# Identity matmuls in TensorE's early gaps: attention with normalized q and k, then a hard-swish feed-forward

## The chip, the cores and the metric

The kernel runs on one core of one Trainium2 chip. The metric is device time in microseconds (us), lower is better. The kernel before took 438.7 us, the median of three runs that lie between 438.64 and 440.98. Engines are named as in the profile: PE is TensorE's matmuls, PEld its weight loads, DVE VectorE, ACT ScalarE, POOL GpSimd, SP the queue that issues most transfers; a small q behind a name (SPq, POOLq) is that engine's queue of transfers.

## The reference

```python
def rmsnorm(x, g):
    rms = np.sqrt(np.mean(x * x, axis=-1, keepdims=True) + 1e-06)
    return x / rms * g
q_n, k_n = (rmsnorm(q, g_q), rmsnorm(k, g_k))
scores = scale * np.matmul(q_n, k_n.transpose(0, 1, 3, 2))
scores = scores - np.max(scores, axis=-1, keepdims=True)
attn = np.exp(scores)
attn = attn / (np.sum(attn, axis=-1, keepdims=True) + 1e-09)
attn_out = np.matmul(attn, v)
x = attn_out.transpose(0, 2, 1, 3).reshape(B * S, H * D)
h = x @ w_in
g = h * np.clip(h + 3.0, 0.0, 6.0) / 6.0
out = g @ w_out
```

There are 8 batches, 12 heads, 448 positions and a head size of 64, so x is 3584 x 768; w_in is 768 x 2048 and w_out 2048 x 768. Inputs and output are 32-bit floats; the kernel's matmuls take bf16.

## The kernel before

**Attention.** Work goes by pairs of heads: 6 pairs a batch, 48 in all. q and k of two pairs are loaded together into one of three buffers (`kq_in`), v into one of three (`v_st`). For a pair, squares are made on ACT or POOL (`square`, L331 and L334), summed on DVE (`stats_sum`, L337), turned into a factor on ACT (`stats_rstd`, L345 and L348) and multiplied in, nearly always on POOL (`normalize`, L353). PE transposes the pair (`transposes`, L367, eight matmuls with the identity), DVE or ACT copies the two halves out of the accumulators (`put_q` L385, `put_k` L303). From pair 14 on transposing DMAs do that instead. Scores are matmuls of 448 columns into two accumulator buffers `sc` (`burst` L395, `rests` L402), ACT takes the exponential into `eT` (L408), PE weighs v with it (`weigh`, L429 and L435: per tile one matmul of 130 columns and six of 65, each with its own 128x128 weight load), DVE divides (`divide`, L445 and L446). v is first cast into `vaug` (`cast_v`, L303 or L307) on whichever engine the planner picks. The result is transposed (`x_out`, L464, or a DMA, L468) and copied into `xT` (L475).

**Feed-forward.** For a batch whose x is complete, `h_mm` (L479) multiplies w_in with `xT`, six matmuls of 448 columns for each of 16 blocks of d_ff; ACT and DVE apply the gate (L485, L490); `y_mm` (L498) multiplies with w_out. One block is special: `h_early` (L588) computes the first block of the first batch piece by piece, one matmul as each pair's x arrives, into the accumulator bank `m_r[0]` (profile name `m`). A bank has 512 columns of 32 bits, of which every user takes columns 0 to 447 or fewer. Pair transposes of x of the first batch go to the other bank, `m_r[1]`.

**What sets the order.** The order of every engine's instructions is fixed when the program is built. `Plan.run` (L140) steps a clock of its own, in ns, over the operations that are ready, with a planned price for each, and calls for each engine the one with the lowest key; what it calls is emitted in that order. Feed-forward matmuls stand in two lanes (`h`, `y`) and are taken when PE has nothing of attention to do or when a credit has run out. Each engine then runs its list in order, and waits by semaphores for the operands. PE is filled from pairs, from `h_early`, and later from the lanes; until the first batch's x is complete there is nothing in the lanes, and the planned clock jumps on (`if not best: now = min(soon)`, L171).

**Weights.** They are loaded by POOL's queue: w_in in five loads (`load_w_in`, L313), the first three after the third group of pairs, w_out in four (L318). POOL's list has its normalizations, squares and casts between these.

**The identity.** POOL makes it at the start (`make_identity`): a memset and one select that ends 2.39 us after the span's start.

Of the kernel before, what the change touches and what calls it, by code (L numbers as in the profile page):

```python
# [28 lines left out]
class Op:  # L29
# [4 lines left out]
    def __init__(self, key, ways, deps, lag, size):  # L34
        self.key, self.ways, self.lag, self.size = key, ways, lag, size
        self.deps = {id(d): d for d in deps if d is not None}
        self.next, self.end, self.time = [], None, 0.0
        self.early = {}
        self.load = False
        self.bank = None  # L40
        self.readers = []
        for d in self.deps.values():
            d.next.append(self)
        self.left = len(self.deps)
# [19 lines left out]
class Plan:  # L64
# [6 lines left out]
    ISSUE, LAND, RATE = {"SP": 600, "ACT": 600, "POOL": 900}, 1700, 270.0  # L71

    STEADY, SLACK, EARLY = 110e3, 500, 3000

    def __init__(self, share):
        self.free = {e: 0.0 for e in ("PE", "ACT", "DVE", "POOL", "SP", "pipe")}
        self.known, self.todo = [], 0
        self.lanes, self.row, self.banks = {"h": [], "y": []}, [], []
        self.share, self.credit = share, 0.0

    def add(self, key, ways, deps=(), lag=0, size=0, hold=False):
        op = Op(key, ways, deps, lag, size)
        op.left += hold
        self.todo += 1
        if op.left == 0:
            self.known.append(op)
        return op
# [52 lines left out]
    def run(self):  # L140
        now = 0.0
        while self.todo or self.row or any(self.lanes.values()):
            soon = [t for t in self.free.values() if t > now]
            best = {}
            for op in self.known:
                t = op.time
                if op.bank is not None:
                    free = After(op.bank).end
                    if free is None:
                        continue  # L150
                    t = max(t, free + self.HOP)
                if t > now:
                    soon.append(t)
                    continue
                engine, ns, fn = min(op.ways, key=lambda w: max(self.free[w[0]], now) + w[1] * (
                    self.PRICE.get(w[0], 1.0) if op.key[0] >= self.FAIR else 1.0))
                if self.free[engine] <= now and (engine not in best or op.key < best[engine][0].key):
                    best[engine] = (op, ns, fn)
            if self.free["PE"] <= now and ("PE" not in best or self.credit < 0):
                if not self.row:  # L160
                    pick = self.next_item(now, soon)
                    if pick:
                        it, bank = pick
                        for lane in self.lanes.values():
                            if lane and lane[0] is it:
                                lane.pop(0)
                        it.bank, bank[1] = bank, it.out
                        self.row = list(it.ops)
                if self.row:
                    best["PE"] = (self.row[0], *self.row[0].ways[0][1:])  # L170
            if not best:  # L171
                now = min(soon)
            for engine, (op, ns, fn) in best.items():
                if op.key is None:
                    self.row.pop(0)
                    share = next((self.share[i] for i in range(0, len(self.share) - 1, 2)
                                  if it.place < self.share[i + 1]), self.share[-1])
                    self.credit = min(self.credit + ns * share, 2000.0)
                else:
                    self.known.remove(op)  # L180
                    self.todo -= 1
                    if engine == "PE":
                        self.credit = max(self.credit - ns, -2000.0)
                self.begin(op, engine, ns, fn, now)
        return now
# [3 lines left out]
def kernel(  # L189
# [11 lines left out]
    nc = tc.nc  # L201

    B, H, S, D = q.shape
# [26 lines left out]
    identity = const.tile([P, P], BF16, name="identity")  # L230
# [29 lines left out]
    plan = Plan(share=(2.0, 1.0, 0.65, 3.0, 0.45))  # L260
# [217 lines left out]
    def h_mm(b, f, kt, m):  # L478
        nc.tensor.matmul(  # L479
            out=m[:, 0:S], lhsT=w_in_sb[:, kt, f * P:(f + 1) * P], rhs=xT[:, kt, b % NX, x_slot(b)],  # L480
            start=(kt == 0), stop=(kt == NKT - 1),
        )

    def relu(m, t):
        nc.scalar.activation(  # L485
            out=t[:], in_=m[:, 0:S], func=RELU, bias=0.5, scale=1.0 / 6.0,
        )

    def gate(b, f, m, t):
        nc.vector.scalar_tensor_tensor(  # L490
            out=gT[:, f, (b % 2) * S:(b % 2 + 1) * S], in0=t[:], scalar=1.0,
            in1=m[:, 0:S], op0=A_MIN, op1=A_MULT,
        )
# [60 lines left out]
    nrm, vc, tr, pq, pk, wgh, div, xo, px = ([] for _ in range(9))  # L554
# [19 lines left out]
    def h_item(b, f):  # L574
        deps = [w_in_op(f)] + px[HP * b:HP * b + HP]

        deps += y_ops.get(b - 2, [])[-1:] + (y_rest.get(b - 1, []) if b % 2 == 0 else [])
        it = plan.item("h", b + f / NFT, NKT, 189, lambda kt, m: h_mm(b, f, kt, m), deps)
        h_ops.setdefault(b, []).append(it.ops[-1])
        n = len(gate_ops)  # L580
        t = t_r[n % len(t_r)]
        r = add((0, 0), [("ACT", 550, lambda: relu(it.bank[0], t))],
                [it.ops[-1]] + gate_ops[n - len(t_r):n - len(t_r) + 1] * (n >= len(t_r)))
        it.out = add((0, 0), [("DVE", 600, lambda: gate(b, f, it.bank[0], t))], [r])
        gates.setdefault(b, []).append(it.out)
        gate_ops.append(it.out)

    def h_early(f):  # L588

        m, t, mm = m_r[f], t_r[f], None  # L590
        for kt in range(NKT):
            mm = add((kt + 2, 2), [("PE", 189, lambda kt=kt: h_mm(0, f, kt, m))],
                     [px[kt], mm, w_in_op(f)], 165)
        h_ops.setdefault(0, []).append(mm)
        r = add((0, 0), [("ACT", 550, lambda: relu(m, t))], [mm])
        out = add((0, 0), [("DVE", 600, lambda: gate(0, f, m, t))], [r])
        gates.setdefault(0, []).append(out)
        gate_ops.append(out)
        plan.banks.append([m, out])
# [23 lines left out]
    def feed_forward(b):  # L623

        if b:
            ts = (NT, *range(NT)) if b % 2 == 0 else range(NT)
            ys = [(t, c) for t in ts for c in range(DM // YC)]
            if b == 1:
                ys = [(0, 0), (1, 0), (0, 1), (1, 1), (2, 0), (2, 1)]
            for i, (t, c) in enumerate(ys):  # L630
                last = b == B and t == NT - 1
                for j in range(2 if last and c else 1):
                    n = YC // 2 if last and c else YC
                    y_item(b - 1, t, c * YC + j * n, n, b + YLAG + (i + j / 2) / len(ys), last)
        if b < B:
            for f in range(NFT):
                h_early(f) if b == 0 and f < 1 else h_item(b, f)
# [20 lines left out]
    def w_in_op(f):  # L658
        return next(op for end, op in w_in_ops if f * P < end)
# [16 lines left out]
    for p in range(NPAIR):  # L676
        g = p // GP
        if p % GP == 0:
# [21 lines left out]
            for i in range(GP):  # L700
                j, p0 = min(i, len(todo) - 1), p + i
                parts = []
                for part in ((0, 1) if p0 == 0 else (2,)):
                    m = len(squares)
# [133 lines left out]
```

## Time and profile before

| what | value |
|---|---|
| median of three runs | 438.7 us |
| the profiled execution | 439.38 us |
| its span, first to last instruction | 437.6 us |
| mean granted TensorE clock, as recorded | 0.996 |
| matmuls, busy PE | 3520, 409.8 us |
| first matmul on PE | 9.38 us |
| POOL busy from 20 to 40 us | 19.88 of 20 us |
| DMA traffic in all | 64.55 MB, 148 GB/s on average |

The profile shows one execution, in microseconds from the first instruction. A row of the timeline gives start, duration, engine, line, operation, result and operands, the number of instructions merged, and in brackets how long the engine had been idle and what released it. Matmuls overlap, so that their durations include the way through the array; the distance from one start to the next is what a matmul costs in a stream. PEclk is the clock that a throttle granted to TensorE, where it is recorded. Idle time of an engine that nothing waits for costs nothing.

### The profile page before, as it was taken

To read this page: it belongs to the slowest core of one execution; us is meant where nothing else is said; L and a number is where in the kernel's file an instruction comes from. 1 tells how busy PE (TensorE), PEld (TensorE's weight loads), DVE (VectorE), ACT (ScalarE), POOL (GpSimd) and SP (SyncE) were. 2 spreads that over 40 slices of the span, in tenths; PEclk is the share of its full clock that TensorE was granted. 3 is DMA by queue.
4 is the path that set the end of the run, shared out by engine and by line. 5 is a ranking of instruction groups with operands and counts; after the bars stand their busy time and mean duration, and the time that the engine had idled before them with its cause. 6 is when DMAs were issued, how large, how long until landed. Compare 5 with 4: busy or idle time off the path is not lost.

```text
span 437.6 us, 8944 instructions
## 1 busy us (share of the span) xinstructions
PE 409.8 (94%) x3520; PEld 236.5 (54%) x3520; DVE 234.7 (54%) x492; ACT 254.3 (58%) x414; POOL 195.2 (45%) x146
## 2 busy tenths in 40 slices
PE   0677899999999998999999999999999999999997
PEld 0355565555566554555555555555565555555565
DVE  6486777766455557556466366344444253343322
ACT  3886887734877885968778587666643032132100
POOL 3697785596377776859676556311000000000000
PEclk9998999999999999999999999999999999999999
DMA  6999999995978898999999994333211201100022
GB/s 170 267 228 216 221 222 239 250 190 131 237 161 190 204 217 189 201 219 194 227 212 167 191 213 121 73 88 91 61 24 49 72 1 51 59 36 37 25 85 73
DMA packets 126506, 64.55 MB, mean 148 GB/s; under 512 B 77824, under 2 KB 123008, under 8 KB 126464
## 3 DMA queue, kind: packets, MB, share of 16 engines
q1 hardware_dynamic: 117488, 57.24, 57.5%
q0 software_dynamic: 8144, 6.29, 9.2%
q8 instruction: 27, 0.44, 0.4%
q10 hardware_dynamic: 832, 0.46, 0.4%
q14 instruction: 15, 0.12, 0.1%
HBM read 45.61 MB, written 11.01 MB: 129 GB/s over the span
## 4 chain that ended last, share of the span: by engine, by line
PE 82%; DMA 7%; ACT 3%; DVE 3%; SPq 2%; POOL 2%; issue 1%; ACTq 0%; POOLq 0%
PE m L479 18%; PE m L498 17%; PE t_ps L498 9%; PE t_ps L479 8%; PE av L435 7%; PE sc L395 6%; PE sc L498 6%; PE sc L479 4%; DMA kq_in<-in_k_dram 3%; DMA kq<-qk 3%; PE av L429 2%; DMA kq_in<-in_q_dram 2%; PE sc L402 2%; ACT eT L408 2%; DVE ssq L337 1%
## 5 line engine op out<-in xcount | busy, mean ns | idle before, releaser
L408 ACT ACTIVATE eT<-sc 128x896 bf16<-128x896 f32 x168 | 147.2, 915 | 42.2 <-PE sc L395 38.5
L498 PEld LDWEIGHTS <-gT 128*128 128x128 bf16 x912 | 85.5, 98 | 61.7 <-issue 8.9
L479 PE MATMUL m<-xT,w_in_sb 128*128 128x448 bf16 x486 | 109.9, 353 | 1.7 <-DVE xT L475 0.6
L479 PEld LDWEIGHTS <-w_in_sb 128*128 128x128 bf16 x768 | 70.7, 98 | 68.8 <-issue 12.0
L353 POOL TENSOR_TENSOR qk<-kq_in,rstd 128x1024 bf16<-128x1024 f32 x47 | 89.0, 1903 | 41.6 <-DMA kq<-qk 20.8
L498 PE MATMUL m<-w_out_sb,gT 128*128 128x384 bf16 (+1 forms) x480 | 87.3, 324 | 0.0
L334 POOL TENSOR_TENSOR sq<-kq_in 128x1024 f32<-128x1024 f32 x41 | 77.2, 1894 | 13.0 <-DMA kq_in<-in_q_dram 3.6
L490 DVE SCALAR_TENSOR_TENSOR gT<-t_sb,m 128x448 bf16<-128x448 f32 x81 | 49.9, 618 | 41.8 <-ACT t_sb L485 41.4
L485 ACT ACTIVATE t_sb<-m 128x448 f32<-128x448 f32 x81 | 44.1, 546 | 47.9 <-PE m L479 47.2
L337 DVE TENSOR_REDUCE ssq<-sq 128x16 f32<-128x1024 f32 (+1 forms) x49 | 58.1, 1190 | 9.5 <-POOL sq L334 7.5
L435 PE MATMUL av<-vaug,eT 128*128 128x65 bf16 x1152 | 59.6, 196 | 0.0
L435 PEld LDWEIGHTS <-eT 128*128 128x128 bf16 x1152 | 52.8, 100 | 7.2 <-issue 1.6
L498 PE MATMUL t_ps<-w_out_sb,gT 128*128 128x384 bf16 x256 | 46.9, 326 | 0.0
L395 PE MATMUL sc<-kq 64*128 64x448 bf16 x288 | 41.6, 363 | 4.0 <-ACT eT L408 2.5
L429 PE MATMUL av<-vaug,eT 128*128 128x130 bf16 x192 | 43.0, 224 | 2.4 <-ACT eT L408 1.2
L479 PE MATMUL t_ps<-xT,w_in_sb 128*128 128x448 bf16 x192 | 44.5, 352 | 0.7 <-DVE gT L490 0.7
L303 POOL CAST vaug<-v_st 128x512 bf16<-128x512 f32 x33 | 20.3, 620 | 55.0 <-PE av L435 46.6
L445 DVE RECIPROCAL rden<-av 128x4 f32<-128x4 f32 x96 | 17.3, 180 | 48.8 <-PE av L435 47.1
L446 DVE TENSOR_TENSOR xn<-av,rden 128x256 bf16<-128x256 f32 x96 | 40.7, 424 | 3.3
L374 ACT ACTIVATE kq<-kq,gprime 128x448 bf16<-128x448 bf16 x34 | 22.8, 670 | 14.2 <-DMA kq<-qk 14.2
L498 PE MATMUL sc<-w_out_sb,gT 128*128 128x384 bf16 (+1 forms) x176 | 29.1, 319 | 0.0
L485 ACT ACTIVATE t_sb<-t_ps 128x448 f32<-128x448 f32 x32 | 17.5, 547 | 19.7 <-PE t_ps L479 18.5
(50 smaller groups left out, 225.0 us busy)
## 6 DMA issues: line engine op xcount, KB each, us to landing
v_st<-in_v_dram SPq DMA_DIRECT2D x24, 384.0 KB, 4.7
kq_in<-in_k_dram SPq DMA_DIRECT2D x23, 384.0 KB, 4.5
kq_in<-in_q_dram SPq DMA_DIRECT2D x23, 384.0 KB, 4.8
out_dram<-y_sb SPq DMA_DIRECT2D x23, 384.0 KB, 2.6
w_out_sb<-in_moe_w_out_dram POOLq DMA_DIRECT2D x4, 768.0 KB, 19.1
w_in_sb<-in_moe_w_in_dram POOLq DMA_DIRECT2D x3, 768.0 KB, 16.2
out_dram<-y_sb SPq DMA_DIRECT2D x9, 192.0 KB, 2.7
v_st<-in_v_dram SPq DMA_DIRECT2D x48, 32.0 KB, 4.3
```

What stands on the lines that cost most here:

```text
L334: eng.tensor_tensor(out=sq, in0=x, in1=x, op=A_MULT)
L337: nc.vector.tensor_reduce(out=ssq_r[(p // GP) % 2][:, p % GP, :, which(part)].rearrange("p h a t -> p h (a t)"), in_=sq_r[m][:, :, which(p ...
L353: eng.tensor_tensor(out=qk_r[p % NQ][:].rearrange("p a t h d -> p h (a t) d"), in0=raw(p, 2), in1=rstd_r[(p // GP) % 2][:, p % GP].rearran ...
L395: nc.tensor.matmul(out=sc[:, h, 0:S], lhsT=kT_r[p % NK][rows, t * P:(t + 1) * P], rhs=qT_r[p % NK][rows], start=True, stop=True,)
L408: nc.scalar.activation(out=e2_r[d % NE][:, :, 0:S], in_=sc_r[i][:, :, 0:S], func=EXP, bias=0.0, scale=1.0,)
L429: nc.tensor.matmul(out=av, lhsT=rest[:, cols], rhs=va[:, 3].rearrange("p h d -> p (h d)"), start=True, stop=False, skip_group_check=True,)
L435: nc.tensor.matmul(out=av[:, h * W:(h + 1) * W], lhsT=e[t][h][:, cols], rhs=va[:, t, h], start=False, stop=(t == NT - 1 and h == 1), skip_ ...
L446: nc.vector.tensor_tensor(out=xn_r[p % NQ][:, t].rearrange("p n (h d) -> p n h d", h=2), in0=av4[:, :, :, 0:D], in1=rden.unsqueeze(3).to_b ...
L479: nc.tensor.matmul(out=m[:, 0:S], lhsT=w_in_sb[:, kt, f * P:(f + 1) * P], rhs=xT[:, kt, b % NX, x_slot(b)], start=(kt == 0), stop=(kt == N ...
L485: nc.scalar.activation(out=t[:], in_=m[:, 0:S], func=RELU, bias=0.5, scale=1.0 / 6.0,)
L490: nc.vector.scalar_tensor_tensor(out=gT[:, f, (b % 2) * S:(b % 2 + 1) * S], in0=t[:], scalar=1.0, in1=m[:, 0:S], op0=A_MIN, op1=A_MULT,)
L498: nc.tensor.matmul(out=m[:, 0:n], lhsT=gT[:, f, c0:c0 + P], rhs=w_out_sb[:, f, c:c + n], start=(f == 0), stop=(f == NFT - 1),)
```

## The change

The planner gets a filler. From 3000 ns of its own clock on, and until the last matmul of `h_early` has been planned, whenever PE is free and no operation is ready for it, the planner emits one matmul of the identity with 64 columns of the identity, and counts PE busy for 56 ns (before 6000 ns of the planned clock) or 36 ns (after). Its result goes to columns 448 to 511 of the bank that `h_early` uses, which nothing reads. The flag `start` is set until the first pair's x is planned, and not after.

```diff
+    WARM = 3000
...
+        self.fill = self.cold = None
...
                 if self.row:
                     best["PE"] = (self.row[0], *self.row[0].ways[0][1:])
+            if "PE" not in best and self.free["PE"] <= now and now >= self.WARM and self.cold.end is None:
+
+                self.fill()
+                self.free["PE"] = now + (56 if now < 2 * self.WARM else 36)
+                soon.append(self.free["PE"])
             if not best:
                 now = min(soon)
...
+    def fill(m, first):
+
+        nc.tensor.matmul(out=m[:, S:S + D], lhsT=identity[:], rhs=identity[:, 0:D], start=first, stop=False,
+                         skip_group_check=True)
...
         h_ops.setdefault(0, []).append(mm)
+        plan.fill, plan.cold = lambda: fill(m, px[0].end is None), mm
```

In the built program this adds 578 matmuls, each with a weight load of the identity, to PE's list. The order of all other instructions, on PE and on the other engines, is as before. The added ones stand, by number: 94 ahead of the first transposes; 34 after them; 42 after the first scores; 33 after the second pair's transposes; 33 ahead of the first `rests`; 52 ahead of the first `weigh`; 50 ahead of the first `x_out`; and 240 in smaller groups of 1 to 26 up to the `rests` that run at 48.62 us in the profile of before.

## The prediction

> **What bounds the kernel now.** I read the page first: TensorE's share, then its slices.
>
> ```profile
> PE 409.8 (94%) x3520; PEld 236.5 (54%) x3520; DVE 234.7 (54%) x492; ACT 254.3 (58%) x414; POOL 195.2 (45%) x146
> ...
> PE   0677899999999998999999999999999999999997
> ...
> PEclk9998999999999999999999999999999999999999
> ```
>
> TensorE ends the kernel: from slice 6 on it hardly rests, and the waits of PE show 4.7 us of idle time after 50 us, all before 227 us. The change touches only the first five slices (0 to 48.6 us), where PE waits. What counts is therefore how much sooner PE reaches the dense phase, which begins with the six matmuls at 52.42 us.
>
> Next the table by stretches of 3.41 us, laid to the one change of clock that is recorded. (Columns: stretch, length, busy time and count of PE, PEld, DVE, ACT, POOL, granted clock, DMA share, GB/s.)
>
> ```profile
> 18.09:21.50 3.41, 2.45 (x24) 1.63 (x25) 1.32 (x3) 3.09 (x7) 3.41 (x3) 1.00 1.07 280
> 21.50:24.91 3.41, 2.89 (x39) 2.50 (x38) 2.89 (x7) 2.44 (x6) 3.41 (x2) 1.00 1.02 264
> ...
> 31.74:35.15 3.41, 1.96 (x27) 1.29 (x27) 2.23 (x5) 3.04 (x4) 3.41 (x3) 1.00 1.16 185
> 35.15:38.57 3.42, 2.93 (x30) 2.33 (x28) 1.52 (x6) 1.25 (x2) 3.40 (x4) 0.50 1.28 226
> ```
>
> One stretch is recorded at clock 0.50: 35.15 to 38.57. It follows a stretch with PE busy for 1.96 of 3.41 us (57%). The clock before 24.91 is printed as 1.00, but the durations deny it:
>
> ```profile
> 23.84 0.54 PE L435 MATMUL av<-vaug,eT 128*128 128x65 bf16 x6
> 24.19 0.30 PE L429 MATMUL av<-vaug,eT 128*128 128x130 bf16 x1
> ```
>
> ```profile
> 32.16 0.35 PE L435 MATMUL av<-vaug,eT 128*128 128x65 bf16 x6
> 32.36 0.22 PE L429 MATMUL av<-vaug,eT 128*128 128x130 bf16 x1
> ...
> 37.11 0.55 PE L479 MATMUL m<-xT,w_in_sb 128*128 128x448 bf16 x1 [0.49 <-DMA w_in_sb<-in_moe_w_in_dram]
> 37.45 1.06 PE L367 MATMUL t_ps<-identity,qk 128*128 128x128 bf16 x8
> 38.31 0.48 PE L479 MATMUL m<-xT,w_in_sb 128*128 128x448 bf16 x1
> 38.72 0.55 PE L395 MATMUL sc<-kq 64*128 64x448 bf16 x4
> 39.21 0.23 PE L429 MATMUL av<-vaug,eT 128*128 128x130 bf16 x1
> ```
>
> From one start to the next, six matmuls of 65 columns, each with its weight load, take 0.35 us at first (58 ns each) and 0.20 us later (33 ns). So PE ran at half clock from 9.38 to 24.91 and from 35.15 to 38.57. Stretches with 85% and 86% busy were followed by full clock, those with 72% and 57% by half.
>
> Last, who else is at its limit before 52 us:
>
> ```profile
> 17.46:28.72 11.26, 8.96 (x102) 6.07 (x101) 7.69 (x18) 9.83 (x17) 11.17 (x6) 1.00 0.99 254
> 28.72:40.90 12.18, 9.50 (x107) 6.18 (x107) 8.45 (x21) 8.53 (x15) 12.16 (x12) 0.86 1.13 207
> ```
>
> POOL is busy for 11.17 of 11.26 and 12.16 of 12.18 us. It issues w_in's first load at 28.72, and PE waits for that load until 37.11. Whatever PE gains earlier is lost in that wait.
>
> **Part by part.** The change removes nothing and moves nothing: the order on all engines is the same but for 578 pairs (weight load of the identity, matmul of 64 columns) among PE's instructions. The nearest row is the 65-column matmul: 33 ns at full, 58 ns at half clock, so 19 to 34 us of new PE work in all.
>
> *First run, 94 fills.* They need only the identity, done at 2.39 us. 94 x 58 ns = 5.5 us ends at 7.8 us, before the first transposes at 9.38. On the path: nothing. The clock should rise during it; 7.8 to 9.38 then stays empty, which can cost one more half-clock stretch, since 57% busy was enough to lose the clock.
>
> *194 fills, 10.2 to 19.05* (34, 42, 33, 33, 52). The gaps of before are 1.16 + 0.94 + 0.39 + 1.18 + 1.07 = 4.74 us. At full clock the fills take 6.4 us, but the real work between saves 4 x 0.4 = 1.6 us. ACT hides more: its squares at 14.22 start when their DMA lands, and it is busy almost without a break to 20.36. One half-clock stretch of 3.41 us holds 59 fills, not 103, so PE loses 1.5 us inside it. I take 0.1 us late for POOL's start at 17.46 (bounds 0 and 1.0).
>
> *290 fills after 19.05.* At full clock av, scores and transposes end sooner than the fills need, up to 37.11, where PE waits 0.49 us anyway. Gain 0: POOL and the load cover it. The new instructions must also be fetched: PE's 7,040 came in the 27 packets of q8, about 260 each, so the change adds 4.4 packets of 1.0 us. At 54.16 and 65.32, where two of them ran, PE shows no idle time; I take 0 (bounds 0 and 1.0, one stall ahead of 19 us). Without that cover the half-clock PE pieces of the chain from 19.05 to 24.82, about 4.8 us of PE, would give back 2.4.
>
> *The stretch 35.15 to 38.57.* The gaps ahead of it (0.43, 0.48, 0.16) get 20, 15 and 9 fills, so PE stays above 85% and the clock should hold. From 37.11 to 38.72 PE does two matmuls of 448 columns (0.39 and 0.41 by their starts) and 8 transposes (0.81): 1.61 us, half of it saved, 0.8. ACT was waiting for just this:
>
> ```profile
> 39.13 2.54 ACT L408 ACTIVATE eT<-sc 128x896 bf16<-128x896 f32 x3 [2.73 <-PE sc L395]
> ...
> 43.90 0.62 POOL L303 CAST vaug<-v_st 128x512 bf16<-128x512 f32 x1 [3.00 <-PE av L435]
> 44.98 3.76 POOL L353 TENSOR_TENSOR qk<-kq_in,rstd 128x1024 bf16<-128x1024 f32 x2 [0.45 <-ACT rstd L348]
> ...
> 48.70 3.74 POOL L334 TENSOR_TENSOR sq<-kq_in 128x1024 f32<-128x1024 f32 x2
> ```
>
> POOL now waits 3.00 us for PE, so the 0.8 passes to 43.90, to 44.98 and to 48.70. Late next is the q load that 48.70 reads: it landed at 47.82, a cap of 0.88. Then sums on VectorE, the gate, and PE at 52.42; the later chain runs from PE to PE and shifts with it.
>
> *Fills after 37.11.* 21 fills (0.69 us) stand in a gap of 0.30, 24 (0.79) in one of 0.60; POOL's 0.45 us wait for ACT hides most. I take 0.15 (bounds 0 and 0.4).
>
> *Two rules weighed.* The row first: the clock fell after a stretch whose longest gap was 0.48 us. The Trainium skill, TensorE: Matmul & The Clock Gate, section "What's actually happening", lets it fall after at least one idle window of about 3.4 us; by that rule idle gaps were not the cause, fills could not hold the clock, and the 0.8 drops out. The trace speaks against it. And 65 columns with their weight load took 33 ns; the same page, "Back-to-back issue gap", gives about 81 ns a matmul for streams of 128 columns with weight loads; as an estimate by that figure the 194 fills would take 15.7 us, and the sum would be some 9 us slower.
>
> **Sum.** -0.8 + 0.1 + 0.15 = -0.55 us. The profiled execution took 439.38 us (span 437.6 and 1.78 around it), so 438.83. The median of the three runs shown is 438.7, 0.68 lower; with the same shift that is 438.15, rounded to **438.2**.
>
> **Rivals.**
> 1. *The clock falls anyway, or the cap comes earlier.* For: the empty 7.8 to 9.38 shows that the plan's gaps aren't the chip's. Against: 85% busy was enough twice. Then only the costs are left: 438.7 + 0.25 = 438.95. The first rule weighed above ends here too.
> 2. *One late half-clock stretch between 10 and 19 us.* POOL has no slack to 40.9, so its bound of 1.0 goes through: 438.7 + 1.0 + 0.15 - 0.8 = 439.05 with the later gain, 439.9 without.
> 3. *Fills outlast their gaps, slower.* It decides where the 194 fills stand: gaps 4.74, savings 1.6, and 1.0 of slack behind av (ACT idle 0.28 at 20.64, av and scores 0.74 sooner) give 7.3 us, or 38 ns a fill. At 33 they fit; at 58, if the small matmuls don't raise the clock, they don't. With 0.86 for transposes and 0.75 for scores at half clock, PE would be 0.64 late at 11.57, 2.0 at 13.44, some 2.6 at the scores that ACT needs at 16.13, 5.6 at 19.05. POOL would be late by 2.6 at 17.46 and about 4.3 at 26.88, which waits for ACT: 443.0 (442 to 445).
> 4. *POOL isn't the bound and PE's half clock is.* The chain of waits does run through PE from 19.05 to 24.82: -2.4 beside the -0.8 gives 435.5. Against: POOL's 11.17 of 11.26.
>
> **How the numbers follow.** Forecast 0.62, first rival 0.14, second 0.09, third 0.10, fourth 0.05. A measurement of this kernel can tell about 0.5% (2.2 us) from no change: the first three cases lie within it (0.85), the fourth above, the fifth below. The range goes down to 437.2 (438.7 less the cap of 0.88, less 0.6 of the 0.68 by which two executions of before differ) and up to 441.0 (the second rival's 439.9 and 1.1 more, about the slowest run shown, 440.98; that holds a fetch stall too). It holds the first three cases; the third and fourth rivals stay outside.
>
> **What would show it.** Right: 65-column matmuls at 33 ns from about 15 us on; no 0.50 from 30 to 40 us; POOL's normalization still near 17.46 and w_in's wait still ending near 37.1; the scores at 38.72 near 37.9; the dense phase near 51.8. Wrong: fills at 58 ns after 16 us, scores of 16.13 late by more than 0.3, w_in landing later, or the first matmul of w_in moved well ahead of 37.

## The result and the profile after

The changed kernel took **443.13 us**, the median of 12 runs (440.6 to 449.0), against 439.38 us for the kernel before in 12 runs beside it (437.48 to 442.32). The ratio is 1.0073, with a 95% interval from 1.0045 to 1.0101; it is worked out without the one execution of 449.0, which ran in a slower state, and is not the quotient of the two medians. The kernel is slower, and outside the range of the prediction. The profiled execution took 445.28 us with a span of 443.5, so 5.9 us more span than before; it lies 2.15 above its median, and the accounts below are those of this one execution.

From the page of the changed kernel: TensorE's share, its slices and clock, and the queue that carries instructions (packets, MB, share of 16 engines).

```profile
PE 424.0 (96%) x4098; PEld 252.9 (57%) x4098; DVE 235.1 (53%) x492; ACT 254.1 (57%) x414; POOL 195.1 (44%) x146
...
PE   6888899999999998899999999999999999999996
...
PEclk9999989999999999999999999999999999999999
...
q8 instruction: 32, 0.52, 0.5%
```

The same queue on the page of the kernel before:

```profile
q8 instruction: 27, 0.44, 0.4%
```

PE is busier in the first slices, as meant: 578 matmuls more. The dip of the clock has moved, from slice 4 to slice 6. Five more packets of instructions came, each of 16,384 bytes, and these turn out to matter.

PE's timeline of the changed kernel (start, duration, line, operation, operands, count, idle time and its releaser):

```profile
2.44 5.20 PE L493 MATMUL m<-identity 128*128 128x64 bf16 x94 [2.44 <-POOL identity masks.py:199]
9.17 0.62 PE L374 MATMUL t_ps<-identity,qk 128*128 128x128 bf16 x8 [1.53 <-DVE qk L360]
...
17.62 1.68 PE L493 MATMUL m<-identity 128*128 128x64 bf16 x52
19.21 0.23 PE L436 MATMUL av<-vaug,eT 128*128 128x130 bf16 x1
...
38.97 0.36 PE L486 MATMUL m<-xT,w_in_sb 128*128 128x448 bf16 x1 [0.68 <-DMA w_in_sb<-in_moe_w_in_dram]
...
39.96 0.55 PE L402 MATMUL sc<-kq 64*128 64x448 bf16 x4
...
55.67 2.23 PE L486 MATMUL m<-xT,w_in_sb 128*128 128x448 bf16 x6 [2.39 <-DVE gT L502]
```

The fills cost what was predicted: the first 94 end at 7.64, and the 52 from 17.62 to 19.21 take 31 ns each. PE is 0.16 us late at 19.21 against 19.05. But the wait for w_in ends at 38.97 instead of 37.11, and the six matmuls that open the dense phase come at 55.67 instead of 52.42, after a wait of 2.39 us. Among PE's waits the profile names none for instructions.

POOL's timeline of the changed kernel, and after it three rows of the kernel before:

```profile
17.62 1.90 POOL L360 TENSOR_TENSOR qk<-kq_in,rstd 128x1024 bf16<-128x1024 f32 x1
21.01 1.89 POOL L341 TENSOR_TENSOR sq<-kq_in 128x1024 f32<-128x1024 f32 x1 [1.48 <-PE t_ps L374]
...
30.27 2.54 POOL L320 DMA_DIRECT2D w_in_sb<-in_moe_w_in_dram  x3
...
51.94 3.74 POOL L341 TENSOR_TENSOR sq<-kq_in 128x1024 f32<-128x1024 f32 x2 [1.94 <-DVE kq L310]
```

```profile
17.46 1.90 POOL L353 TENSOR_TENSOR qk<-kq_in,rstd 128x1024 bf16<-128x1024 f32 x1 [0.27 <-ACT rstd L348]
19.32 1.90 POOL L334 TENSOR_TENSOR sq<-kq_in 128x1024 f32<-128x1024 f32 x1
...
28.72 2.54 POOL L313 DMA_DIRECT2D w_in_sb<-in_moe_w_in_dram  x3
```

POOL's normalization starts at 17.62, 0.16 later than before, but the square that followed it without a pause now waits 1.48 us. The brackets name PE and, later, VectorE, as the last event seen; the landings say otherwise. The q load that the square at 21.01 reads landed at 20.80 (before: 18.93), 0.21 us ahead of it. In four of the experiments below (e3, e4, e7, e8) the same square also starts 0.21 us behind this load, and in e8 the bracket names it. The one that the square at 51.94 reads landed at 51.78 (before: 47.82). From the first comes w_in's issue, 1.55 us late, and so the 38.97. From the second comes the 55.67, over VectorE's sum and the gate that stands behind it; VectorE's timeline of the changed kernel:

```profile
53.87 1.22 DVE L344 TENSOR_REDUCE ssq<-sq 128x16 f32<-128x1024 f32 x1 [2.07 <-POOL sq L341]
55.00 1.14 DVE L502 SCALAR_TENSOR_TENSOR gT<-t_sb,m 128x448 bf16<-128x448 f32 x2
```

So **loads land late**. What stands beside the step is the second packet of instructions, which ran at 16.94 for 1.23 us. SP's queue at that time in the changed kernel, and the same two issues before; then the queues of the changed kernel from 16.5 to 18.5 (packets, MB, share of 16 engines):

```profile
16.55 2.01 SPq L307 DMA_DIRECT2D v_st<-in_v_dram  x2
```

```profile
15.97 1.25 SPq L300 DMA_DIRECT2D v_st<-in_v_dram  x2
```

```profile
q1 hardware_dynamic: 842, 0.46, 92.7%
q8 instruction: 1, 0.02, 3.9%
```

A single packet of 16 KB takes 3.9% of 16 engines for 2 us, as much as one engine for 1.25 us, while the loads' packets take 93%. (Such shares add up packets that overlap, so that they can pass 100%.) On the trace, four of the loads' packets of 768 bytes that began beside it, at 17.05, 17.11, 17.21 and 18.11, took 0.58, 0.70, 1.27 and 0.38 us, where the median of the others is 0.036. By themselves these four prove little: in the kernel before, with no instruction packet near, five packets that began between 17.4 and 18.2 took 0.42 to 0.75 us, and in the changed kernel one at 13.05 took 1.06. What stands out is the step in the landings, and SP's issue: the k load due at 17.29 landed 1.95 us late, the one due 0.26 ahead of it 0.54 late, and SP's second issue took 1.37 us instead of 0.61.

### The profile page after: what moved, and what is told of

It reads as the page before. It is cut to its first block, busy times and chain, and to the rows that moved or that the text cites. A ratio compares the mean times of both kernels' runs of the same rounds, so it can differ in the third digit from the quotient of the medians.

```text
span 443.5 us, 10100 instructions
## 1 busy us (share of the span) xinstructions
PE 424.0 (96%) x4098; PEld 252.9 (57%) x4098; DVE 235.1 (53%) x492; ACT 254.1 (57%) x414; POOL 195.1 (44%) x146
## 4 chain that ended last, share of the span: by engine, by line
PE 74%; DMA 13%; SPq 5%; DVE 3%; POOL 2%; issue 1%; ACT 1%; ACTq 0%; POOLq 0%
PE m L486 17%; PE m L510 17%; PE t_ps L510 9%; PE t_ps L486 7%; PE sc L510 6%; PE av L442 6%; DMA kq_in<-in_q_dram 5%; PE sc L402 5%; DMA kq<-qk 4%; PE sc L486 4%; DMA v_st<-in_v_dram 3%; POOL sq L341 2%; PE av L436 2%; PE sc L409 2%; DVE ssq L344 1%; SPq L307 1%
## 5 line engine op out<-in xcount | busy, mean ns | idle before, releaser
L442 PE MATMUL av<-vaug,eT 128*128 128x65 bf16 x1152 | 58.4, 194 | 0.0
L442 PEld LDWEIGHTS <-eT 128*128 128x128 bf16 x1152 | 51.6, 98 | 6.8 <-issue 1.2
L402 PE MATMUL sc<-kq 64*128 64x448 bf16 x288 | 40.7, 358 | 2.8 <-ACT eT L415 2.5
L452 DVE RECIPROCAL rden<-av 128x4 f32<-128x4 f32 x96 | 17.3, 180 | 47.7 <-PE av L442 46.1
L497 ACT ACTIVATE t_sb<-t_ps 128x448 f32<-128x448 f32 x32 | 17.5, 547 | 19.7 <-PE t_ps L486 18.6
## 6 DMA issues: line engine op xcount, KB each, us to landing
w_in_sb<-in_moe_w_in_dram POOLq DMA_DIRECT2D x3, 768.0 KB, 17.2
```

What stands on the lines that cost most here:

```text
L402: nc.tensor.matmul(out=sc[:, h, 0:S], lhsT=kT_r[p % NK][rows, t * P:(t + 1) * P], rhs=qT_r[p % NK][rows], start=True, stop=True,)
L442: nc.tensor.matmul(out=av[:, h * W:(h + 1) * W], lhsT=e[t][h][:, cols], rhs=va[:, t, h], start=False, stop=(t == NT - 1 and h == 1), skip_ ...
L497: nc.scalar.activation(out=t[:], in_=m[:, 0:S], func=RELU, bias=0.5, scale=1.0 / 6.0,)
```

## The experiments

All of them keep the order of the other instructions on every engine as it is before, but for the second. Nothing of the computation is left out in any: fills write columns that are not read, or that are overwritten later. The theories: **A**, the packets that fetch instructions, pulled forward into the time of the first loads, hold up the data; **B**, the fills among the matmuls of w_in, from 37 us on, cost PE time; **C**, PE's streaming at full clock disturbs the loads; **D**, the weight loads of the fills, which read SBUF, do. The table stands ahead for the runs that can be compared: instructions added to PE, packets of instructions in the first 56 us and where the early ones began, the landing of the q load that POOL's square reads (18.93 before), the start of the dense phase, and the ratio. In e1 and e5 POOL came to that square only after the load, at 20.40 and 19.56, and did not wait for it.

| run | added | packets to 56 us | q landed | dense phase | ratio [95%] |
|---|---|---|---|---|---|
| before | 0 | 3: 26.3, 41.3, 54.2 | 18.93 | 52.42 | |
| changed | 1156 | 7: 8.0, 16.9, 22.5, 28.0, ... | 20.80 | 55.67 | 1.0073 [1.0045, 1.0101] |
| e1_short_stop | 944 | 6: 7.9, 18.6, 23.4, 27.9, ... | 19.80 | 55.46 | 1.0124 [1.0073, 1.0176] |
| e3_one_col | 944 | 6: 6.3, 17.6, 24.7, 28.6, ... | 21.85 | 57.69 | 1.0141 [1.0104, 1.0177] |
| e8_small_reads | 944 | 6: 6.2, 17.2, 24.3, 28.8, ... | 21.21 | 58.24 | 1.0099 [1.0060, 1.0138] |
| e7_until_av | 576 | 5: 8.1, 16.9, 22.3, ... | 20.61 | 52.80 | 1.0036 [1.0013, 1.0059] |
| e4_first94 | 188 | 3: 7.9, 31.5, 46.1 | 20.67 | 52.81 | 1.0000 [0.9975, 1.0026] |
| e5_long_same_order | 120 | 3: 20.8, 38.5, 48.0 | 19.35 | 51.78 | 0.9996 [0.9971, 1.0021] |

**e1_short_stop**: the fills end at the first matmul of w_in, 472 instead of 578.

```diff
-        plan.fill, plan.cold = lambda: fill(m, px[0].end is None), mm
+        plan.fill, plan.cold = lambda: fill(m, True), first_mm
```

> The changed kernel, but the fills end where the first matmul of w_in is planned: 472 fills of 64 columns instead of 578, 944 added PE instructions, some 3.7 packets of 256. Theory A (the packets that fetch PE's instructions hold up the loads of q, k and v): the third group's q lands near 20.5 us as in the changed kernel (18.9 before), w_in's first load near 38.5, time about 3 us above before. Rival B (only the fills among the w_in matmuls hurt): the time falls back to within 0.5 us of before. Rival C (a TensorE that streams or runs at full clock slows the loads): as A, so this run is the partner of the next two.

444.95 us against 438.88, 6 us more where about 3 were expected. Without a fill behind 37 us the kernel is as slow as with them, so B is not the main cause. But e1 is no clean partner of the change. The clock was granted at half from 8.53 to 15.35, and there the fills took 53 ns and outlasted their gaps: the second pair's transposes came at 15.23 instead of 13.44. POOL's timeline of this run:

```profile
18.54 1.90 POOL L360 TENSOR_TENSOR qk<-kq_in,rstd 128x1024 bf16<-128x1024 f32 x1 [1.31 <-ACT rstd L355]
```

So POOL was 1.08 us late at its normalization because of the clock, and w_in's issue 0.96 late (29.68), before any late load held POOL. The trace adds a second way in which a late issue costs. Beside the packet at 27.9 SP's issue at 28.29 takes 1.49 us, and the next q load is issued at 29.83, now behind w_in's 768 KB at 29.68 instead of 0.84 us ahead of them. It lands at 35.17 (before 31.68), and ACT waits (ACT's timeline of this run):

```profile
35.60 1.06 ACT L339 ACTIVATE sq<-kq_in 128x1024 f32<-128x1024 f32 x1 [3.10 <-DMA kq_in<-in_q_dram]
```

w_in itself landed early in this run (36.12, before 37.06; about 38.5 was expected), and PE still came to it only at 39.44: the load of q was the later one. ACT's exponential stands behind this square, and PE waited 2.28 us for it, up to 37.52.

**e2_long_fills**: few and long fills. Each has 448 columns, and the planner counts 376 and 190 ns for it: 88 fills instead of 472.

```diff
-                self.free["PE"] = now + (56 if now < 2 * self.WARM else 36)
+                self.free["PE"] = now + (376 if now < 2 * self.WARM else 190)
...
-        nc.tensor.matmul(out=m[:, S:S + D], lhsT=identity[:], rhs=identity[:, 0:D], start=first, stop=False,
+        nc.tensor.matmul(out=m[:, 0:S].rearrange("p (n d) -> p n d", d=D), lhsT=identity[:],
+                         rhs=identity[:, 0:D].unsqueeze(1).to_broadcast([P, S // D, D]), start=first, stop=False,
```

> As e1, but each fill has 448 columns: 88 fills fill the same gaps, 176 added instructions, 0.7 of a packet. The clock should rise as early as with short fills. Theory A: packets before 56 us fall from 6 or 7 to 4, the third group's q lands by 19.3, w_in by 37.5, time within 1 us of before, perhaps 0.5 below it. Rival C: TensorE streams as much as in e1, so loads land as late as in e1 and the time stays some 3 us above before.

440.31 against 438.88, ratio 1.0042 [1.0015, 1.0069]. Two expectations were missed: the time is 1.4 us above before, not within 1, and w_in landed at 38.31, not by 37.5. The other prices changed the planner's clock and with it the order of real instructions, so the total decides nothing; e5 repeats it without that. What holds regardless: the loads landed within 0.15 us of before's from 9.8 to 24 us, and the first packet of instructions, at 22.6, was followed at once by a q load 1.0 us late (25.20 for 24.21).

**e3_one_col**: as e1, but each fill streams one column instead of 64.

```diff
-        nc.tensor.matmul(out=m[:, S:S + D], lhsT=identity[:], rhs=identity[:, 0:D], start=first, stop=False,
+        nc.tensor.matmul(out=m[:, S:S + 1], lhsT=identity[:], rhs=identity[:, 0:1], start=first, stop=False,
```

> As e1, with the same 944 instructions in the same places, but each fill streams 1 column instead of 64. Theory A: packets as in e1, loads as late as in e1, time 3 us or more above before (more if the clock now stays at half until 25 us). Rival C: hardly any streaming is left, so loads land as before and the time is within 0.5 us of before.

445.64 against 438.88. With 1/64 of the streaming, and PE at half clock until 23.74 (before: 24.91), the q load is 2.9 us late: C falls. The total shows the clock as well as the loads: the dense phase is later still, at 57.69, since PE then stayed at half clock for four stretches on end (stretch, length, busy times, granted clock, DMA share, GB/s; this run):

```profile
27.15:30.57 3.42, 2.31 (x63) 1.90 (x61) 2.24 (x6) 2.62 (x5) 3.04 (x3) 1.00 0.89 233
30.57:44.22 13.65, 13.23 (x183) 9.86 (x182) 8.52 (x19) 8.45 (x14) 12.77 (x12) 0.50 1.06 192
```

**e4_first94**: only the first 94 fills, ahead of the first transposes.

```diff
-        plan.fill, plan.cold = lambda: fill(m, px[0].end is None), mm
+        plan.fill, plan.cold = lambda: fill(m, True), tr[0]
```

> Only the first run of 94 fills ahead of the first transposes; 188 added instructions, 0.7 of a packet. Theory A: one packet moves to about 8 us, the later ones stay apart as before, time 0 to 1 us above before. Rival B and C: no change of the loads after 10 us, time as before. In all theories the clock falls back after the first run and is half again until 20 us or later.

439.14 against 438.88, no difference. One packet came early, at 7.9, and SP's queue shows the price beside it (this run):

```profile
7.72 2.28 SPq L299 DMA_DIRECT2D kq_in<-in_k_dram  x2
```

The two issues took 1.62 and 0.60 us. Later issues are 1.16 us behind, the loads due from 15.4 on land 1.5 late, and q at 20.67. The fills had ended at 6.89, so it is not their running that held these loads. But no other packet followed until 31.5; w_in's wait ended at 38.02, and the dense phase lost only 0.39, as the clock was full from 33.18 on. One early packet delays the loads and does not, alone, move the time.

**e5_long_same_order**: the planner counts as in e1, but only each seventh fill of a run is emitted, with 448 columns: 60 matmuls for nearly the same cover.

```diff
+        plan.run7 += 1
+        if plan.run7 % 7 == 0:
+            nc.tensor.matmul(out=m[:, 0:S].rearrange("p (n d) -> p n d", d=D), lhsT=identity[:],
+                             rhs=identity[:, 0:D].unsqueeze(1).to_broadcast([P, S // D, D]), start=first, stop=False,
+                             skip_group_check=True)
```

> As e1, planned the same, so that the order of all other instructions is that of before (in e2 it was not). Of each run of short fills every seventh is emitted, with 448 columns: 60 fills, 120 instructions, half a packet. Theory A: packets before 56 us at most 4, loads within 0.5 us of before up to 30 us unless a packet meets one that POOL waits for; time within 1 us of before, 5 us below e1. If TensorE's streaming were the cause, the time would stay near e1.

438.65 against 439.19, no difference that can be told; the profiled span is 436.6, 1.0 less than before. The first packet came at 20.8, and up to it the loads land within 0.5 us of before's. PE's timeline of this run, with SP's queue after it:

```profile
37.17 0.35 PE L489 MATMUL m<-xT,w_in_sb 128*128 128x448 bf16 x1
37.80 0.35 PE L489 MATMUL m<-xT,w_in_sb 128*128 128x448 bf16 x1
38.08 0.55 PE L405 MATMUL sc<-kq 64*128 64x448 bf16 x4
...
51.78 1.30 PE L489 MATMUL m<-xT,w_in_sb 128*128 128x448 bf16 x6 [0.50 <-DVE gT L508]
```

```profile
7.74 1.25 SPq L302 DMA_DIRECT2D kq_in<-in_k_dram  x2
```

Here the kernel does what was predicted for the change: w_in landed at 36.90 and its first matmul is at 37.17, the scores are at 38.08 instead of 38.72, the dense phase at 51.78 (predicted: near 51.8). One sign differs: the clock was at half from 28.38 to 31.80, where "no 0.50 from 30 to 40" was forecast; by w_in's first matmul PE had made that good. And though the clock was full from 7.90 to 28.38, POOL issued w_in no earlier (29.06, before 28.72) and PE came to it no earlier (before: 37.11). That speaks against the fourth rival, in which PE's half clock was the bound.

**e6_semaphores**: a test of D. In place of each fill of e1, PE increments a semaphore twice: 944 instructions that read nothing.

```diff
-        nc.tensor.matmul(out=m[:, S:S + D], lhsT=identity[:], rhs=identity[:, 0:D], start=first, stop=False,
-                         skip_group_check=True)
+        for _ in range(2):
+            nc.tensor.sem_inc(idle_sem, 1)
```

> As e1, but each fill is two increments of a semaphore that nobody waits for: the same 944 added PE instructions in the same places, with no matmul, no weight load and no read of SBUF. Theory A: packets as in e1, loads late as in e1, time 3 to 7 us above before. Rival D (the weight loads of the fills, which read SBUF, hold up the loads that write it): loads as before, time within 1 us of before. The clock stays as in before in both.

555.36 us against 439.19, ratio 1.2635, and no answer: the increments were far from free. PE's timeline of this run:

```profile
40.15 0.93 PE L402 MATMUL sc<-kq 64*128 64x448 bf16 x4 [9.62 <-issue]
52.98 1.01 PE L374 MATMUL t_ps<-identity,qk 128*128 128x128 bf16 x8 [11.90 <-issue]
```

68 increments stand ahead of the first row and 84 ahead of the second: 141 ns each. PE came to w_in at 151.55 us, and nothing else of the run can be compared.

**e7_until_av**: the first 288 fills, up to the first `weigh`.

```diff
-        plan.fill, plan.cold = lambda: fill(m, px[0].end is None), mm
+        plan.fill, plan.cold = lambda: fill(m, True), wgh[0][0]
```

> The changed kernel with its first 288 fills only (up to the first weighing of v): 576 added instructions, 2.25 packets, between e4 (0.7 packets, time as before) and e1 (3.7 packets, 6 us above). Theory A: two packets more than before ahead of 30 us, time 1 to 4 us above before. Rival E (it is the fills after 19 us that hurt, by standing ahead of real work): time as in e4.

440.81 against 439.19, ratio 1.0036 [1.0013, 1.0059]: between e4 and the change. Its third early packet is at 22.3, and none follows until 40.9. The loads are 1.5 us late near 20 us, and recover to 0.7 at the one due at 47.82.

**e8_small_reads**: D again. As e1, with 32x32 weights and one column: the same 944 instructions with a sixteenth of the reading.

```diff
-        nc.tensor.matmul(out=m[:, S:S + D], lhsT=identity[:], rhs=identity[:, 0:D], start=first, stop=False,
+        nc.tensor.matmul(out=m[0:32, S:S + 1], lhsT=identity[0:32, 0:32], rhs=identity[0:32, 0:1], start=first, stop=False,
```

> The same 472 fills at the same places as in the first experiment, so again 944 instructions more on TensorE, but each takes 32x32 weights and one column instead of 128x128 and 64: a sixteenth of what the weight loads read from SBUF, and 1/64 of the columns. Theory of the fetches (the extra packets of instructions among the loads of the first 55 us hold back the data): nothing changes in what is fetched, so the loads land 1 to 3 us late from the first or second extra packet on, w_in's first matmul stands at 39 to 42 us, and the time is 4 to 7 us above before (ratio 1.009 to 1.016). Rival (the fills' reads of the identity from SBUF, and the writes behind them, hold back the loads): the loads land within 0.3 us of before's, w_in at 37 to 38, and the time is within 1.5 us of before. At 32x32 and one column TensorE may stay at half clock early; by the run with one column of full weights that alone cost nothing that could be told from the fetches.

444.11 against 439.09. The loads are late as with full weights (q by 2.28 us, in e3 by 2.91), so D falls. POOL's timeline of this run, where the bracket now names the load itself, and SP's queue:

```profile
21.42 1.89 POOL L341 TENSOR_TENSOR sq<-kq_in 128x1024 f32<-128x1024 f32 x1 [1.01 <-DMA kq_in<-in_q_dram]
```

```profile
17.46 1.98 SPq L307 DMA_DIRECT2D v_st<-in_v_dram  x2
```

The load landed at 21.21, again 0.21 us ahead of the square. Two numbers missed what was expected: some loads were up to 3.75 us late, not 1 to 3, and w_in's first matmul is at 43.19, not at 39 to 42, though w_in landed at 39.23. PE was at half clock from 30.43 to 44.08 and busy for 13.32 of these 13.65 us; the last 4 us are the clock's, as in e3, and not the loads'.

**Taken together.** In each of these runs but e6, the landings are within 0.5 us of before's until about the first packet (but for one in e8, 0.82), and step up behind it, wherever it lies: 6.2, 8.0, 20.8 or 22.6. Some of that is made good again before the next packet, in e1 nearly all. Up to 31 us each packet, before's own at 26.3 too, has a stretched SP issue beside it, of 0.9 to 2.0 us where nearly all others take 0.4 to 0.6. (From 31 us on, issues of up to 3.75 us stand in the kernel before too, with no packet for PE near.) That holds with fills of 448, 64 or 1 columns and with full or small weights. A is supported; that the packet is the cause of the stretched issue, and not a companion, rests on this agreement. How much of a late landing is the shared engine and how much the late issue was not separated. The time is not in simple proportion to the packets: 5 in the first 56 us cost 0.36%, 6 cost 0.99 to 1.41%, 7 cost 0.73%, with intervals that overlap; and e1, e3 and e8 also lost time to the clock.

The traces show one more thing on which the loss hangs: **the order of two issues near 29 us.** Before, SP issues the last q load of its group at 27.88 and the v load behind it at 28.58, both ahead of POOL's issue of w_in at 28.72. In the changed kernel two of SP's issues take 1.62 and 1.39 us beside the packets at 22.5 and 28.0, and the v load is issued at 30.82, behind w_in at 30.27. The q load ahead of w_in is 2.26 us late; the v load behind it is 4.62 late, and so the loads after it. The same step stands in e1 (1.64 to 3.49) and e3 (3.21 to 4.29), where loads also fell behind w_in. In e4, e7, e5 and e8 the v load stayed ahead, by 0.08 to 0.27 us, and the lateness fell (1.34 to 1.11, 1.71 to 0.62, 0.33 to none) or hardly grew (e8, 2.66 to 2.90). No experiment changed this order alone, so it is read from the traces and not tested.

No version beat the kernel before. The best, e5, gains 0.64 us at the dense phase and has an interval of 0.25% to either side, 1.1 us, so it would take more than these runs to tell.

## Why the prediction was wrong

- **Fills' price and the first run: right, with luck.** 94 fills end at 7.64 (predicted 7.8), and at full clock a fill takes 31 ns (predicted 33). The empty 7.8 to 9.38, which "can cost one more half-clock stretch", did not: the clock is recorded as full from 8.08 on. That was luck in where the stretches lay. In e1, e4 and e7, with the same 94 fills, the clock rose earlier, at 5.1 to 5.9, and fell back to half at 8.5 to 9.3.
- **The 194 fills: right here, and the size by chance.** POOL's normalization is 0.16 late (predicted 0.1), but not for the fills: ACT's squares begin at 14.39 instead of 14.22, behind a q load that landed 0.16 late. The third rival, fills that outlast their gaps, needed 58 ns a fill; its time, 443.0, is close to the measured one by chance. In e1, with the clock at half, such fills did hold PE up.
- **The 290 fills, "gain 0: POOL and the load cover it": right for PE, and the cover itself moved.** In e5, with the loads in time, full clock before 28 us gained nothing. In the changed kernel POOL's square went from 19.32 to 21.01 and w_in's issue from 28.72 to 30.27.
- **The step that failed is the fetch of the new instructions**: "the change adds 4.4 packets of 1.0 us. At 54.16 and 65.32, where two of them ran, PE shows no idle time; I take 0 (bounds 0 and 1.0, one stall ahead of 19 us)". The count was right (5) and so was the duration (0.9 to 1.24 us). It asked only whether PE would starve, and PE never did. It did not ask what else the packets' engines were carrying. Nor did it ask where the packets would fall: with 1156 instructions in the first 49 us, not the five alone but all that follow come earlier, so that four lie before 30 us, where before had one. There the table of stretches already showed the DMA share at 1.02 to 1.16. The bound of 1.0 was a price for PE; the lateness that followed is 1.87 us at the q load, 1.55 at w_in's issue and 3.25 at the dense phase, where a gain of about 0.6 was forecast (51.8). Nor did it ask what a stretched issue does to the order of the loads: the step from 2.26 to 4.62 us of lateness stands where the v load fell behind w_in.
- **The stretch 35.15 to 38.57: right.** The clock held; from w_in's first matmul to the scores PE took 0.99 us instead of 1.61, and in e5, where the loads were in time, 0.64 of the predicted 0.8 reached the dense phase.
- **The fills after 37.11: right.** Laid side by side with the same matmuls of before, those of the changed kernel are 1.24 us late at 39 us and 1.37 late at 51: 0.13, predicted 0.15. In e4, e5 and e7, without these fills, that lateness did not change there.
- **The cap: the right chain with the wrong sign.** "Late next is the q load that 48.70 reads: it landed at 47.82". That load, then the sums, the gate and PE are the path by which 3.96 us of lateness became 3.25. PE's wait for w_in, 1.86 us late, is the smaller part: 0.62 of it was made good by the faster clock, and the rest was overtaken by this load.
- **A term that was not in the sum:** PE's wait of 2.39 us made a new stretch of half clock later. From the table of stretches of the changed kernel:

```profile
35.39:38.80 3.41, 2.00 (x35) 1.37 (x32) 3.16 (x8) 3.27 (x5) 3.40 (x4) 1.00 1.30 228
...
52.46:55.87 3.41, 1.02 (x12) 0.37 (x9) 2.00 (x3) 2.39 (x4) 3.22 (x2) 1.00 1.21 211
55.87:59.28 3.41, 3.41 (x19) 1.29 (x18) 2.54 (x5) 1.34 (x3) 0.00 (x0) 0.50 1.21 223
```

 PE is busy all through it. The same matmuls are 3.25 us late ahead of it and 4.81 late behind it, so it costs 1.56 us. PE stays 4.81 late until 160 us. The other 1.1 of the 5.9 us of span arise behind that. There PE's lateness in e4, e5 and e7 moves too, by 1.8 us one way (e4, 160 to 180 us) and 1.2 the other (e7, up to 300 us), so they are not put down to the change.
- **The two rules of the Trainium skill.** The gate: before's stretch with 57% busy and the one with 30% above lost the clock, and neither was one whole idle window, so the rule of the Trainium skill as the prediction cites it does not describe the fall here. Nor does a threshold of busy time describe it: in e5 a stretch with 54% busy kept the clock (7.90 to 11.32) and another with 54% lost it (24.97 to 28.38). The gap: in the kernel before eight transposes of 128 columns, each with its weight load, took 0.46 us from 25.29 to 25.75, which is 57 ns each, not the 81 of the Trainium skill.

The range's upper end, 441.0, allowed for one stall. The share for slower, 0.10, was carried by rivals that all sat on PE. None of them happened in the profiled execution of the change (in e1 the second did: half clock until 15.35, POOL 1.08 late), and the mechanism that did happen sat on a resource that the prediction had printed as full.

## What to carry to other kernels

Instructions are data too: when a change adds some hundreds of them to an engine, find on the instruction queue how many make a packet, place the packets on the timeline, and look at what the DMA engines carry there. If loads are on the path at that time, use few long instructions instead of many short ones: with 60 fills of 448 columns the clock held from 35.15 to 38.57 as it did with 578 of 64 (though it was at half from 28.38 to 31.80), and the loads stayed within 0.5 us until the first packet. Where two queues issue loads close together, look also whether a delay of one swaps their order: here 0.55 us behind w_in went with 2.4 us more lateness. A resource that is full counts as bound for everything that the change sends through it, also for traffic that no line of the kernel issues.

## What the runs showed of the hardware

- One packet of 16 KB of instructions came for about 256 of PE's instructions (8196 in 32 packets in the changed kernel) and took 0.9 to 1.24 us there, up to 1.82 in e3; single loads landed 0.5 to 2 us late behind it. The Trainium skill, Runtime: NRT & Kernel Launch, "Instruction fetch mechanics", gives the same block of 256 instructions and calls the cost of crossing one mostly hidden. For PE the traces agree, with no wait of PE that the profile puts down to it; the loads beside it, on which that sentence says nothing, did pay.
- Every recorded state of the clock that ended within a run lasted 3.41 us or a multiple of it. With matmuls of 64 or more columns it was lost after stretches in which PE was busy for 30% (the change), 37% (e1), 46% (e4 and e7), 54% (e5) and 57% (before), and kept after 52% (e2, 36.71 to 40.12), 54% (e5), 59 and 61% (both the change). With fills of one column it was lost after 68 and 77% (e3 and e8), and stayed at half while PE's record read 97% busy for 13.65 us. So what the gate counts is not the busy time that the profile prints; that short streams count for less fits e3 and e8, but was not tested by itself.
- A semaphore increment on PE took 141 ns (e6), more than four times a matmul of 64 columns with its weight load (31 ns at full clock).
